# Pooled attention and a gated conv FFN: pooled keys and values in flat 128-row tiles, no conv on TensorE, some gates by sigmoid

## The chip, the cores and the metric

One core of a Trainium2 chip. The metric is the device time of one execution in microseconds; lower is better. The inputs are fp32 in HBM and the output is fp32; inside, the kernel works in bf16 with fp32 accumulation in PSUM.

## The reference

Eight batches, eight heads, 576 tokens, head size 64. Keys and values are averaged over groups of 8 tokens, so each head has 72 pooled keys. The attention output, with the heads side by side (512 wide), is the input of a gated feed-forward block.

```python
k_p = k.reshape(B, H, 72, 8, D).mean(axis=3)
v_p = v.reshape(B, H, 72, 8, D).mean(axis=3)
attn = softmax(q @ k_p.T / 8)                      # 576 x 72 per head
x = (attn @ v_p)                                   # heads side by side: B x 576 x 512
h = maximum(x @ w_in, 0)                           # 512 -> 1024
conv = cw[0]*h[s-1] + cw[1]*h[s] + cw[2]*h[s+1]    # along the tokens, per channel
out = (h * sigmoid(conv)) @ w_out                  # 1024 -> 512
```

## The kernel before

The kernel first makes a list of steps (`Planner.add`), each with an engine or a choice of engines, an estimated duration, a priority from `PARAMS`, what it reads and writes, and the PSUM slot that it takes. `Planner.order` then puts the steps in order, greedily, by those estimates, and the instructions are issued in just that order. Each engine works through its own queue in order. PSUM has three slots of two banks (tiles called psfA or psbA) and two slots of one bank (psfB, psbB). Gaps that the planner expects on TensorE in the first 60 us are filled with matmuls on zeros (`warm`, L266).

For each batch b the steps are these.

- **Loads.** `load_k`, `load_q` and `load_v` fetch with casting DMAs from GpSimd's queue (POOL). k_b holds the keys as 96 rows by 6, one row being the 8 tokens of a pooled key; v_b holds 72 rows by 8 heads. q_b holds the queries as flat tokens, 128 partitions of 36 tokens each. All three have two buffers, for even and odd batches. `weights_in` fetches w_in in four parts, `weights_out` w_out in two.
- **Pooling.** `attn_k` (L450 to L485) adds 512 elements to 256, 128 and 64 on DVE and transposes the sums into kT2; `attn_v` (L499 to L511) does the same additions for vaug, which has a 65th column of 8.0 that gives the row sums of the softmax.
- **Queries.** `attn_q` transposes q_b in 18 blocks (L523) and copies the result to qT (L529).
- **Scores.** `attn_s`: for each head two matmuls on 64 rows, of 72 by 288 each (L548), and one exp of 72 x 576 on ACT (L560); in batch 0 in three column parts, so 24 exps there and 56 in the other batches.
- **AV.** `attn_av`: for each of five token tiles eight matmuls of 65 columns (L580), the reciprocal of the row sums (L589), the normalisation xx on DVE (L593), four transposes (L607, with the permutation `perm` that undoes the token order) and a copy to xT (L613) by ACT or DVE.
- **mm1.** `mm1` (L652): eight matmuls of 288 columns for each of eight blocks f of 128 channels; relu on ACT (L658) into hT. Batch 0 is done in two column parts (L629, L636).
- **Conv and gate.** For two blocks at a time. A block in `PARAMS["off"]` goes through `conv_off`: the two outer taps are multiplied by DVE or ACT (L677, L675; the taps are divided by the middle one), two additions on DVE (L683, L689), a tanh on ACT (L694). The other ten blocks of the 64 go through `conv_pe`: six matmuls with diagonal matrices dw (L731) and a tanh from PSUM (L738). The gate is 0.5 (1 + tanh(z/2)): hT already holds half of h, DVE adds 1 (`tg1`, L711) and multiplies into gT (L717).
- **mm2.** Two batches share gT, 1152 tokens in nine tiles; `mm2` (L757) takes eight matmuls of 512 columns for each tile; ACT or DVE copies to osb (L784), and SyncE's queue (SP) stores (L789).

tanh, exp, relu and copy stand in one table of ACT, which is loaded once (L529 ACT_TABLE_LOAD). The batches overlap: loads run two batches ahead, attention one batch ahead of the feed-forward block.

Of the kernel before, what the change touches and what calls it, by code (L numbers as in the profile page):

```python
# [16 lines left out]
    "off": [(3, 5, 7), (0, 1, 2, 3, 6, 7), (0, 1, 2, 4, 5, 6, 7), (0, 1, 2, 3, 4, 5, 6, 7), (0, 1, 2, 3, 4, 5, 6, 7),  # L17
        (1, 2, 3, 4, 5, 6), (0, 1, 2, 3, 4, 5, 6, 7), (0, 1, 2, 3, 4, 5, 6, 7)],
    "acc": [0, 0, 0, 0, 0, 0, 0, 0],
    "bias": {"cp": 0.0323, "qT": -0.1231, "xt": 0.043, "kz": -0.1719, "oe": 0.0913},  # L20
    "ld0": [3.1628, -11.898, 6.0356, 17.1517],
    "ps0": [-11.2829, 7.5625, 41.439],
    "k": [-5.9822, -1.1583, -4.5734, -3.831, -6.5225, -2.7562, -4.2806, 15.1584],
    "q": [-0.1097, -9.2157, -9.8568, 3.1829, -4.6592, -3.0682, -1.5265, -8.4274],
    "v": [24.0425, -11.1807, 29.0547, 7.0183, 0.6186, 5.6688, -7.284, 39.6168],
    "s": [-6.9912, -16.7009, -0.9318, -0.6168, -3.6961, -1.0376, -0.9093, 1.2171],
    "ds": [3.8131, -0.3704, 0.0793, 0.7876, 1.3609, 0.4842, 0.2144, -4.845],
    "av": [-16.159, 1.1624, 8.4491, 2.1533, -4.2703, 4.1242, 4.9518, -37.1794],
    "conv": [4.8877, 4.2326, 2.864, 6.3276, 6.3981, 1.7124, -22.1068, 5.7406],
    "mm2": [25.5649, 32.1081, 13.6617, 18.3164, 23.0188, 19.8928, 18.2176, 20.5433, 24.0796, 28.9795, 21.0736,  # L30
        23.1375, 15.9486, 13.2485, 25.641, 4.8532, 20.6698, 5.4106, 10.0051, 16.9607],
# [3 lines left out]
ROW = 0.05  # L35
# [3 lines left out]
class Op:  # L39
    __slots__ = ("i", "name", "eng", "dur", "lat", "deps", "prio", "fn", "take", "give", "nbytes", "done", "users", "after")  # L40


class Planner:
# [4 lines left out]
    KINDS = {"qT": "BA", "kT": "BA", "xt": "BA", "cw": "BA", "o": "B", "sc": "A", "sc0": "A", "av": "A", "h": "A", "h0": "BA", "c": "A"}  # L48
    DMA_RATE = 330e3
# [3 lines left out]
    QUOTA = {"sc": 2, "o": 2}  # L53

# [6 lines left out]
    def add(self, name, eng, dur, fn, reads=(), writes=(), prio=0.0, lat=None, take=None, give=None, nbytes=0, after=None):  # L61
# [5 lines left out]
        o.fn, o.prio, o.take, o.give, o.nbytes = fn, prio, take, give, nbytes  # L67
# [8 lines left out]
        for k in writes:  # L76
            if k not in reads:
                self.writers[k] = [o.i]
                self.readers[k] = []
            else:  # L80
                self.writers[k] = [o.i]
                self.readers[k] = []
        deps.discard(o.i)
# [3 lines left out]
        o.done = None  # L87
        self.ops.append(o)
# [4 lines left out]
    def order(self):  # L93
# [14 lines left out]
        dma_free = 0.0  # L108
        busy = {}
        out = []  # L110
        while avail:
            best = None
            per = {}
            for i, t in avail.items():
# [9 lines left out]
                for e, d in o.eng.items():  # L124
                    s = max(st, free.get(e, 0.0))
                    f = s + d
                    if e == "ACT" and len(o.eng) > 1:
                        f += self.bias.get(o.name.split(".")[0][:2], 0.0)
                    if cand is None or f < cand[0]:
                        cand = (f, s, e)  # L130
# [10 lines left out]
            d = o.eng[e]  # L141
            del avail[i]
# [13 lines left out]
            if o.nbytes:  # L156
                dma_free = max(dma_free, s + d) + o.nbytes / self.DMA_RATE
                o.done = dma_free + (self.DMA_LAT if o.lat is None else o.lat)
            else:
                o.done = s + d + (self.LAT[e] if o.lat is None else o.lat) + self.SEM  # L160
# [12 lines left out]
        return out  # L173


@with_exitstack
def kernel(
# [19 lines left out]
    A = 16  # L197
    J = S // A
    KR = 96
    KT = H * Sp // KR  # L200

# [9 lines left out]
    perm = st("perm", [P, P], BF16)  # L211
    w_in = st("w_in", [P, n_dc, d_ff], BF16)
# [6 lines left out]
    dw = st("dw", [P, n_fb, 3, P], BF16)  # L219

    k_b = [st(f"k_b{i}", [KR, KT, 512], BF16) for i in range(2)]
    v_b = [st(f"v_b{i}", [Sp, H, 512], BF16) for i in range(2)]
    q_b = [st(f"q_b{i}", [P, J, D], BF16) for i in range(2)]
    kp1 = st("kp1", [KR, KT, 256], BF16)
    kp2 = st("kp2", [KR, KT, 128], BF16)
    ksum = st("ksum", [KR, KT, 2, D], BF16)
    vp1 = st("vp1", [Sp, H, 256], BF16)
    vp2 = st("vp2", [Sp, H, 128], BF16)
    vaug = [st(f"vaug{i}", [Sp, H, D + 1], BF16) for i in range(2)]
    kT2 = [st(f"kT2{i}", [P, H * Sp], BF16) for i in range(2)]  # L230
    qT = [st(f"qT{i}", [P, J // 2, P], BF16) for i in range(2)]
    attnT = [st(f"attnT{i}", [Sp, H, S], BF16) for i in range(2)]
# [3 lines left out]
    hT = [st(f"hT{i}", [P, n_fb, S + 4], BF16) for i in range(2)]  # L236
# [5 lines left out]
    OFF = PARAMS["off"]  # L242

# [13 lines left out]
    def warm(gap, x, prev):  # L257
        n = min(int((gap - 0.05) / 0.06), 100)
        if x is not None:
            t = pp.tile([P, 2 if x[0] == "A" else 1, 512], FP32, name=f"psw{x[0]}", tag=f"ps{x[0]}{x[1]}")[:, 0, 0:P]  # L260
        elif prev is not None and prev.take is not None and prev.take[0] == "sc0":
            t = slot(prev.take)[:, 0, 384:512]
        else:
            return
# [6 lines left out]
    def flat_tokens(src, b):  # L271
        return src[b].rearrange("h t d -> (h t d)").rearrange("(p e) -> p e", p=P)

    def rows_k(b):
        return k[b].rearrange("h (s p) d -> (h s) (p d)", p=8).rearrange("(t p) e -> p t e", p=KR)

    def rows_v(b):
        return v[b].rearrange("h (s p) d -> s h (p d)", p=8)
# [3 lines left out]
    def setup(b):  # L282
        pass

    QG = [(0, 4), (4, 12), (12, 18)]

    def load_q(b, parts, prio):
        m = b % 2
        for x, (c0, c1) in enumerate(QG if parts > 1 else [(0, J // 2)]):
            def fn(e, c0=c0, c1=c1):  # L290
                nc.gpsimd.dma_start(
                    out=q_b[m][:, 2 * c0:2 * c1, :],
                    in_=flat_tokens(q, b)[:, 2 * c0 * D:2 * c1 * D].rearrange("p (j d) -> p j d", d=D),
                )
            pl.add(f"ldq{b}.{x}", "POOL", 0.6, fn, writes=[("q", m, y) for y in ((x,) if parts > 1 else (0, 1, 2))],
                   prio=prio + (PARAMS["ld0"][x] if b == 0 else 0.0), nbytes=P * 2 * (c1 - c0) * D * 4)

    def load_k(b, prio):
        m = b % 2
        if b == 0:  # L300
            for i in range(2):
                def fn(e, i=i):
                    nc.gpsimd.dma_start(out=k_b[0][:, 3 * i:3 * i + 3, :], in_=rows_k(0)[:, 3 * i:3 * i + 3, :])
                pl.add(f"ldk0.{i}", "POOL", 0.75, fn, writes=[("kl", i)], prio=prio, nbytes=H * S * D * 2)
        elif PARAMS["acc"][b]:
            accumulate(b, "k", k_b, rows_k(b), prio)
        else:
            def fn(e):
                nc.gpsimd.dma_start(out=k_b[m], in_=rows_k(b))
            pl.add(f"ldk{b}", "POOL", 0.9, fn, writes=full_keys("k", m) + first(b, "k"), prio=prio, nbytes=H * S * D * 4)  # L310

    def half(b, full):
        x = 256 * ((b // 2 + 1) % 2)
        return full[b % 2][:, :, x:x + 256]

    def half_keys(b, name):
        return [(name, b % 2, (b // 2 + 1) % 2)]

    def full_keys(name, m):
        return [(name, m, 0), (name, m, 1)]  # L320

    def first(b, name):
        return [(name + "l", 0), (name + "l", 1)] if b in (2, 4) else []

    def accumulate(b, name, full, src, prio):
        n = 2 ** PARAMS["acc"][b]
        w = 512 // n
        keys = half_keys(b, name)
        for i in range(n):
            def fn(e, i=i):  # L330
                kw = {} if i == 0 else {"accum_op": OP.add}
                nc.gpsimd.dma_start(out=half(b, full)[:, :, 0:w], in_=src[:, :, i * w:(i + 1) * w], **kw)
            pl.add(f"ld{name}{b}.{i}", "POOL", 0.9, fn, reads=keys if i else [], writes=keys + (first(b, name) if i == 0 else []), prio=prio,
                   nbytes=int(H * S * D * 4 / n * 1.7), lat=5.0)

    def load_v(b, prio):
        m = b % 2
        if PARAMS["acc"][b]:
            return accumulate(b, "v", v_b, rows_v(b), prio)

        n = 2 if b == 0 else 1
        for i in range(n):
            def fn(e, i=i):
                c = slice(i * H // n, (i + 1) * H // n)
                nc.gpsimd.dma_start(out=v_b[m][:, c, :], in_=rows_v(b)[:, c, :])
# [493 lines left out]
    with tc.manual_schedule():  # L839
        prev = None  # L840
        for s, e, d, o in pl.order():
# [3 lines left out]
            if e == "PE":  # L845
                prev = o
# [31 lines left out]
```

## Time and profile before

| | |
|---|---|
| median of 3 runs | 210.06 us (209.61 to 210.35) |
| span of the profiled execution, first to last instruction | 208.8 us |
| time of the profiled execution itself | not listed apart from the three runs; the median is 1.26 us above the span |
| mean granted TensorE clock | 0.998 |
| busy PE, DVE, ACT, POOL | 200.5, 177.1, 169.9, 33.7 us |
| DMA packets, bytes | 20794, 26.02 MB |

The profile lists for every group of instructions its line in the kernel, what it writes and reads by the kernel's names, partitions by elements, the count, the busy time of the group and the mean duration of one in ns, then the idle time of the engine just before them and what ended it. PE is the matmul part of TensorE and PEld its weight loads. A digit in the slices is the busy share of an engine in a fortieth of the span, in tenths. The chain of waits goes back from the last instruction, at each step to what released it.

### The profile page before, as it was taken

Reading aid. Unit: us, or ns where it says so; the run is one execution under the profiler, and the core shown is the slowest. Engines: PE = TensorE matmul, PEld = TensorE weight load, DVE = VectorE, ACT = ScalarE, POOL = GpSimd, SP = SyncE. Lnnn points to the kernel's source line nnn. Section 1 sums busy time; section 2 is a strip of 40 time slices with the busy share of each in tenths; the row PEclk is TensorE's granted clock in tenths of the full one; section 3 lists DMA queues with packets and bytes.
Section 4 is the critical chain, followed back from the end, with each engine's and each line's share of the span. In section 5 each row is a group of like instructions: output and inputs, shape, how many; then the busy total and the mean of one; then the engine's idle time right before and its main releaser. Section 6 shows DMA issues by size and latency. Waiting matters only on the chain.

```text
span 208.8 us, 4761 instructions
## 1 busy us (share of the span) xinstructions
PE 200.5 (96%) x1917; PEld 135.2 (65%) x1917; DVE 177.1 (85%) x396; ACT 169.9 (81%) x305; POOL 33.7 (16%) x70
## 2 busy tenths in 40 slices
PE   8999899899999889999999999999999999999993
PEld 8987684687466666757565586547645767764432
DVE  1576589699999999999999999998997799999601
ACT  2056579969999997799999999999999878999431
POOL 7859951111303110010100100000000000000000
PEclk9999999999999999999999999999999999999999
DMA  5999999999999999309732280102202202102425
GB/s 76 160 198 206 204 206 210 201 198 195 155 142 224 170 249 186 77 5 144 166 119 102 33 179 6 53 0 100 96 9 100 104 0 104 50 0 102 154 100 201
DMA packets 20794, 26.02 MB, mean 125 GB/s; under 512 B 2444, under 2 KB 15268, under 8 KB 20772
## 3 DMA queue, kind: packets, MB, share of 16 engines
q0 software_dynamic: 15648, 16.26, 49.5%
q1 hardware_dynamic: 5124, 9.45, 12.0%
q8 instruction: 15, 0.25, 0.5%
q14 instruction: 7, 0.06, 0.1%
HBM read 32.52 MB, written 9.44 MB: 201 GB/s over the span
## 4 chain that ended last, share of the span: by engine, by line
PE 87%; ACT 8%; DVE 3%; issue 0%; ACTq 0%
PE psfB L757 30%; PE psfA L652 27%; PE psfA L548 5%; PE pswA L266 5%; ACT attnT L560 4%; PE psfA L580 4%; PE psfA L731 3%; PE psbB L607 3%; PE psfB L629 2%; PE psbB L523 2%; PE pswB L266 2%; DVE xx L593 1%; PE psbA L607 1%; PE psbB L480 1%; ACT osb L784 1%; ACT tg L738 1%
## 5 line engine op out<-in xcount | busy, mean ns | idle before, releaser
L757 PE MATMUL psfB<-w_out,gT 128*128 128x512 bf16 (+1 forms) x296 | 66.8, 373 | 0.5 <-ACT osb L784 0.5
L652 PE MATMUL psfA<-xT,w_in 128*128 128x288 bf16 x448 | 60.7, 286 | 0.3 <-ACT attnT L560 0.2
L652 PEld LDWEIGHTS <-w_in 128*128 128x128 bf16 x448 | 42.1, 98 | 12.7 <-issue 1.3
L757 PEld LDWEIGHTS <-gT 128*128 128x128 bf16 x296 | 27.7, 98 | 29.6 <-issue 1.3
L560 ACT ACTIVATE attnT<-psfA 72x576 bf16<-72x576 f32 (+3 forms) x80 | 39.8, 549 | 1.9 <-PE psfA L548 1.5
L658 ACT ACTIVATE hT<-psfA 128x576 bf16<-128x576 f32 x56 | 35.5, 652 | 6.3 <-PE psfA L652 5.9
L694 ACT ACTIVATE tg<-cv,cs 128x576 bf16<-128x576 bf16 x54 | 39.9, 777 | 0.8 <-DVE cv L689 0.8
L677 DVE TENSOR_SCALAR cv<-hT,cr 128x576 bf16<-128x576 bf16 x78 | 26.0, 361 | 3.3 <-ACT hT L658 3.1
L593 DVE TENSOR_TENSOR xx<-psfA,rr 128x512 bf16<-128x512 f32 x40 | 26.8, 681 | 0.1
L784 ACT COPY osb<-psfB 128x512 f32<-128x512 f32 x31 | 17.9, 584 | 9.0 <-PE psfB L757 8.7
L717 DVE TENSOR_TENSOR gT<-tg,hT 128x1152 bf16<-128x1152 bf16 x32 | 23.9, 747 | 0.1
L675 ACT ACTIVATE cv<-hT,cr 128x576 bf16<-128x576 bf16 x30 | 22.7, 781 | 0.2
L689 DVE TENSOR_TENSOR cv<-cv 128x1152 bf16<-128x1152 bf16 (+1 forms) x30 | 20.5, 684 | 0.0
L683 DVE TENSOR_TENSOR cv<-cv,hT 128x1152 bf16<-128x1152 bf16 (+1 forms) x30 | 20.4, 681 | 0.0
L548 PE MATMUL psfA<-qT,kT 64*72 64x288 bf16 (+3 forms) x160 | 19.0, 277 | 1.4 <-ACT attnT L560 0.8
L266 PEld LDWEIGHTS <-zero 128*128 128x128 bf16 x216 | 15.2, 110 | 2.6 <-DVE zero L365 1.0
L548 PEld LDWEIGHTS <-kT 64*72 64x72 bf16 x160 | 7.8, 107 | 13.4 <-issue 10.2
L711 DVE TENSOR_SCALAR tg<-tg 128x1152 bf16<-128x1152 bf16 x32 | 14.3, 448 | 1.7 <-ACT tg L694 1.2
L580 PE MATMUL psfA<-vaug,attnT 72*128 72x65 bf16 x320 | 15.5, 194 | 0.3 <-ACT attnT L560 0.3
L529 ACT COPY qT<-psbB 128x512 bf16<-128x512 bf16 (+2 forms) x10 | 7.1, 744 | 9.6 <-PE psbB L523 9.6
L580 PEld LDWEIGHTS <-attnT 72*128 72x128 bf16 x320 | 13.5, 98 | 1.5 <-issue 0.5
L607 PEld LDWEIGHTS <-xx 128*128 128x128 bf16 x160 | 10.7, 97 | 4.8 <-DVE xx L593 1.1
(67 smaller groups left out, 218.4 us busy)
## 6 DMA issues: line engine op xcount, KB each, us to landing
out_dram<-osb SPq DMA_DIRECT2D x15, 512.0 KB, 3.3
k_b<-in_k_dram POOLq DMA_DIRECT2D x7, 576.0 KB, 12.1
q_b<-in_q_dram POOLq DMA_DIRECT2D x7, 576.0 KB, 10.6
v_b<-in_v_dram POOLq DMA_DIRECT2D x7, 576.0 KB, 9.8
out_dram<-osb SPq DMA_DIRECT2D x5, 256.0 KB, 2.0
w_in<-in_moe_w_in_dram POOLq DMA_DIRECT2D x4, 256.0 KB, 10.2
w_out<-in_moe_w_out_dram POOLq DMA_DIRECT2D x2, 512.0 KB, 18.1
k_b<-in_k_dram POOLq DMA_DIRECT2D x2, 288.0 KB, 6.2
```

The lines of the kernel that those rows point to most:

```text
L266: nc.tensor.matmul(out=t, lhsT=zero[:, 0:P], rhs=zero[:, 0:P], start=True, stop=True)
L548: nc.tensor.matmul(out=t[:, par, :], lhsT=kT2[m][64 * par:64 * par + 64, h * Sp:(h + 1) * Sp], rhs=qT[m][64 * par:64 * par + 64, 2 * c0:2 ...
L560: nc.scalar.activation(out=attnT[m][:, h, :].rearrange("p (c i x) -> p i c x", i=2, x=32)[:, :, c0:c1, :], in_=view().rearrange("p i (c x) ...
L580: nc.tensor.matmul(out=a[:, h // 4, c:c + D + 1], lhsT=attnT[m][:, h, u0:u0 + 128], rhs=vaug[m][:, h, :], start=True, stop=True)
L593: nc.vector.tensor_tensor(out=xx[i3].rearrange("p (g h e) -> p g h e", g=2, h=4), in0=av_view()[:, :, :, 0:D], in1=rr[i3].rearrange("p (g ...
L652: nc.tensor.matmul(out=t[:, i, 0:HC], lhsT=w_in[:, c, f * P:(f + 1) * P], rhs=xT[m][:, c, i * HC:(i + 1) * HC], start=(c == 0), stop=(c == ...
L658: nc.scalar.activation(out=hT[m][:, f, 2:S + 2].rearrange("p (i x) -> p i x", i=2), in_=slot(key)[:, :, 0:HC], func=ACT.Relu, scale=0.5)
L675: nc.scalar.activation(out=cv[y][:, kk // 2, z, :], in_=src, func=ACT.Copy, scale=s)
L677: nc.vector.tensor_scalar(out=cv[y][:, kk // 2, z, :], in0=src, scalar1=s, scalar2=None, op0=OP.mult)
L694: nc.scalar.activation(out=tg[i3][:, f % 2, :], in_=cv[y][:, 0, z, :], func=ACT.Tanh, scale=cs[:, f:f + 1])
L717: nc.vector.tensor_tensor(out=gT[(b // 2) % 2][:, fs[0]:fs[0] + 2, o:o + S], in0=tg[i3], in1=hT[m][:, fs[0]:fs[0] + 2, 2:S + 2], op=OP.mult)
L757: nc.tensor.matmul(out=a[:, 0, 0:cols.stop - cols.start], lhsT=g[:, c, t * P:(t + 1) * P], rhs=w_out[:, c, cols], start=(c == 0), stop=(c ...
```

## The change

- Keys and values are pooled as flat rows (head, token): 576 rows in five tiles of 128, the last half empty. The loads of k and v are split in four full tiles and a tail of 64 rows (batch 0 in three transfers).
- Queries are loaded as 72 partitions by 8 heads by 8 tokens into a single q_b, and then regrouped to q2, token before head: by two copies on DVE (or ACT) for batches 0 to 3 and 7, by eight SyncE DMAs of 128-byte pieces for batches 4 to 6 (`PARAMS["rg"]`). Transposes take two heads of 72 tokens, 32 for a batch.
- kz is a block layout of kT for pairs of heads with zeros between. A score tile holds 128 flat keys; one or two pairs of heads are accumulated into it, each by matmuls of 512 and 64 columns with 128 rows. There are five exps of 128 x 576 for a batch, batch 0 included.
- In AV a flat tile of keys can hold rows of up to three heads: vblk holds the pooled values three times, each times a mask (made on POOL) that is one for the rows of that head. Six matmuls of 65, 130 or 195 columns replace eight of 65.
- Every conv block goes off TensorE. The conv matrices dw are no longer made.
- The order of tokens in xT is the natural one, so the copies read and write runs of 128.
- ACT's gate is a sigmoid where the planner has the sigmoid table in place, else 0.5 (1 + tanh): `PARAMS["sw"]` and `Planner.SWITCH` decide. In the built order 42 of the 64 gates are sigmoids, and ten table loads stand on ACT, nine of them inside the stream. `tg1` (now 0.5 x + 0.5) is left out where all the gates of a pair are sigmoids; relu is no longer halved.
- w_in is fetched in two parts. The planner has another model of the DMA queues and an order of loads written out (`PARAMS["seq"]`), and all priorities are new.

The core of the diff:

```diff
+    q_b = st("q_b", [PR, H, TP, D], BF16)
+    q2 = st("q2", [PR, TP, H, D], BF16)
...
+    def regroup(b, pr):
+        n = 2 if b == 0 else 1
+        if PARAMS["rg"][b] == "D":
+            for h in range(0, H, 4):
+                def fn(e, h=h):
+                    copy_on(e)(out=q2[:, :, h:h + 4, :], in_=q_b[:, h:h + 4].rearrange("p h i d -> p i h d"))
+                pl.add(f"qg.{b}.{h}", {"DVE": 0.6, "ACT": 1.8}, 0, fn, reads=[("ql", h // 4)], writes=[("q", 0, h + z) for z in range(4)],
+                       prio=pr + 0.01 * h)
+            return
+        for h in range(H):
+            def fn(e, h=h):
+                nc.sync.dma_start(out=q2[:, :, h, :], in_=q_b[:, h])
...
+        mk = mask.rearrange("p t x d -> p (t x d)")
+
+        def fn(e):
+            nc.gpsimd.memset(mk, 1.0)
+        pl.add("mask0", "POOL", 0.5, fn, writes=["mask"], prio=-50)
+        for x, (base, sg) in enumerate(((Sp, 1), (-1, -1))):
+            def fn(e, base=base, sg=sg):
+                nc.gpsimd.affine_select(out=mk, in_=mk, compare_op=OP.is_ge, fill=0.0, base=base,
+                                        pattern=[[-16 * sg, NT], [-Sp * sg, 3], [0, D + 1]], channel_multiplier=sg)
...
+        def fn(e):
+            nc.vector.tensor_tensor(out=vs, in0=vp2[:, :, 0:D], in1=vp2[:, :, D:2 * D], op=OP.add)
...
+            nc.vector.tensor_tensor(out=vblk[m][:, :, :, 0:D], in0=vs.unsqueeze(2).to_broadcast([P, NT, 3, D]),
+                                    in1=mask[:, :, :, 0:D], op=OP.mult)
...
+    PAIRS = [(0,), (0, 1), (1, 2), (2, 3), (3,)]
...
+            for y, (n0, n1) in enumerate(((0, 512), (512, S))):
+                for c in PAIRS[t]:
+                    w = kz[m][:, 256 * c + (P if t > c else 0):256 * c + (P if t > c else 0) + P]
+                    r = qT[m][:, c]
...
+                    nc.tensor.matmul(out=a[:, y, 0:n1 - n0], lhsT=w, rhs=r, start=c == PAIRS[t][0], stop=c == PAIRS[t][-1])
...
-            for h in range(H):
-                c = (h % 4) * (D + 1)
-                nc.tensor.matmul(out=a[:, h // 4, c:c + D + 1], lhsT=attnT[m][:, h, u0:u0 + 128],
-                                 rhs=vaug[m][:, h, :], start=True, stop=True)
...
+            for s, x0, x1, g, c in ((0, 1, 3, 0, 0), (1, 0, 3, 0, 1), (2, 0, 1, 0, 3), (2, 1, 3, 1, 0), (3, 0, 3, 1, 1), (4, 0, 1, 1, 3)):
+                nc.tensor.matmul(out=a[:, g, c * w:(c + x1 - x0) * w], lhsT=attnT[m][:, s, u0:u0 + 128],
+                                 rhs=vblk[m][:, s, x0:x1, :].rearrange("p x d -> p (x d)"),
...
-                out=xT[m].rearrange("p c (a j) -> p c a j", j=J)[:, :, :, 8 * t:8 * t + w],
-                in_=slot(key2)[:, 0, 0:512].rearrange("p (c a j) -> p c a j", c=4, a=A)[:, :, :, 8 - w:8],
...
+            copy_on(e)(out=xT[m][:, :, 128 * t:128 * t + w],
+                       in_=slot(key2)[:, 0, 0:512].rearrange("p (c a) -> p c a", c=4)[:, :, 0:w])
...
+                half = not pl.ops[gi[z0]].mode
+                nc.scalar.activation(out=tg[i3][:, zs[z0]:zs[z0] + z1 - z0, :], in_=cv[y][:, 0, z0:z1, :],
+                                     func=ACT.Tanh if half else ACT.Sigmoid, scale=cs[:, g:g + 1] if half else cn[:, 1, g:g + 1])
...
+                nc.vector.tensor_scalar(out=t, in0=t, scalar1=1.0, scalar2=0.5, op0=OP.add, op1=OP.mult)
```

And in the parameters:

```diff
-    "off": [(3, 5, 7), (0, 1, 2, 3, 6, 7), (0, 1, 2, 4, 5, 6, 7), (0, 1, 2, 3, 4, 5, 6, 7), (0, 1, 2, 3, 4, 5, 6, 7),
-        (1, 2, 3, 4, 5, 6), (0, 1, 2, 3, 4, 5, 6, 7), (0, 1, 2, 3, 4, 5, 6, 7)],
...
+    "sw": [0, 1, 1, 1, 0, 1, 0, 1],
...
+    "rg": "DDDDSSSD",
```

## The prediction

> **What bounds the kernel now.** I read the page first: busy shares, then the slices.
>
> ```profile
> span 208.8 us, 4761 instructions
> PE 200.5 (96%) x1917; PEld 135.2 (65%) x1917; DVE 177.1 (85%) x396; ACT 169.9 (81%) x305; POOL 33.7 (16%) x70
> DVE  1576589699999999999999999998997799999601
> ACT  2056579969999997799999999999999878999431
> PE 87%; ACT 8%; DVE 3%; issue 0%; ACTq 0%
> ```
>
> One digit is 5.2 us. DVE is nearly full from the ninth digit (42 us) to 195 us, ACT not far behind. PE's busy time counts matmul latency and warm-up matmuls on zeros, so I price PE by starts. The chain in order of time does that:
>
> ```profile
> 22.46 0.55 PE psfA L266 x7
> 23.02 0.65 PE psfB L629 x4
> ...
> 33.81 4.35 ACT attnT L560 x8
> ...
> 48.93 1.96 PE psfA L652 x16
> ...
> 78.02 1.73 PE psfB L757 x8
> ...
> 185.71 13.39 PE psfB L757 x62
> 199.17 0.59 ACT osb L784
> ```
>
> So 128x512 costs 0.2165 us (1.73/8), 128x288 0.1225 (1.96/16), 0.42 ns a column. The first real layer-1 matmul (mm1) starts at 22.85 by the timeline, its last layer-1 matmul ends at 185.71; then only mm2 is left. The groups by form give ACT and DVE:
>
> ```profile
> L694 ACT ACTIVATE tg<-cv,cs 128x576 bf16<-128x576 bf16 x54 | 39.9, 777 | 0.8 <-DVE cv L689 0.8
> L560 ACT ACTIVATE attnT<-psfA 72x576 bf16<-72x576 f32 x56 | 33.3, 646 | 0.2 <-PE psfA L548 0.2
> L677 DVE TENSOR_SCALAR cv<-hT,cr 128x576 bf16<-128x576 bf16 x78 | 26.0, 361 | 3.3 <-ACT hT L658 3.1
> L711 DVE TENSOR_SCALAR tg<-tg 128x1152 bf16<-128x1152 bf16 x32 | 14.3, 448 | 1.7 <-ACT tg L694 1.2
> L499 DVE TENSOR_TENSOR vp<-v_b 72x2048 bf16<-72x2048 bf16 x7 | 8.5, 1215 | 0.0
> L529 ACT ACT_TABLE_LOAD x1 | 1.3, 1283 | 0.7 <-PEq L862 0.7
> ```
>
> Neighbours overlap: eight exps take 4.46 us, the last one whole, so 0.535 each against 0.646; a tanh pair 1.44, so 0.665. I take 0.115 off each ACT mean and 0.075 off each DVE mean (0.448 starts the next after 0.37). Counts by order times these prices give the work before: PE 174.2 (mm1 62.7, mm2 62.3, transposes 19.6, scores 12.3, AV 10.0, conv 7.4), DVE 174.3, ACT 161.1 us. PE holds 150.5 of it between 22.85 and 185.71, 162.9 us long: 12.4 us of gaps, about 4 of them before 44.6 us.
>
> **The change, engine by engine.** Counts come from the built order.
>
> PE. Sixty conv matmuls go: -7.4. Scores become 64 pairs of 512 and 64 columns, 64 x 0.247 = 15.8, against 112 x 0.0925 + 1.9 = 12.3: +3.5. AV becomes 40 tiles of 130, 195 and 65 columns twice, 0.35 each by column, 14.0 against 320 x 0.031 = 10.0: +4.0. The 256 transposes of q at 72 columns (0.034) cost 8.7 against 144 x 0.057 = 8.3; those of k +0.2. PE: 175.0, +0.8. So taking the conv off PE only pays for the flat tiles.
>
> ACT. Exps 80 to 40: 21.3 against 34.8, -13.5. Nine table loads inside the stream at 1.28: +11.5; of the 64 gates 42 use sigmoid, priced like tanh from SBUF (+1.3 in all). Copies of xT 14 to 33: +8.3. Copies of kz +2.4, of osb -1.8, the rest -0.2. Sum +8.0: 169.1.
>
> DVE. Outer-tap multiplies 78 to 99: +6.0; their adds, all 1152 wide now: +6.3. The gate's add 32 to 11: -7.8. Copies of xT 26 to 7: -5.9; of osb +2.4; of k -0.5. Pooling on 128 rows, 1280, 640 and 320 elements where 2048 and 1536 were: -7.2 by the slope (1.215-0.422)/1536 us. New is the masked copy vblk, 960 elements, eight times. No row has its two strides at once; by the same slope 0.65, by twice the element time 1.15. The old vaug write, also 65 apart, cost 0.422 like a plain 512, so I take 0.65: +4.6. New too are ten regrouping copies of q, 2048 elements: 0.70 by the slope from the multiply of 576 to the add of 1152, 1.2 by the tensor_tensor row of 2048. It reads one tensor out of SBUF, as the multiply and the add do: 0.70, +6.2. Small things +0.5. DVE: 178.9, +4.6. Its set-up memsets and the first batch's two regroupings, about 3.5 us, fall before 20 us, where DVE idles; so the load afterwards hardly grows.
>
> Queues. On POOL k0 and v0 come in three transfers and q0 in two, then two mask passes (0.29 for 128 columns, so 1 to 2 us each for 975), and w_in stands behind them, issued near 12 us instead of 6.6. It is not needed before 21 us, and the 1.77 MB ahead of it keep the DMA busy to about 13; without that cover mm1 waits for it, some 2 us. q_b is one buffer now, so the load of the next q, and v's behind it on POOL, wait for the regrouping of this one; POOL already waits 24.5 us for kp to free k_b by the waits, and nothing on the chain is released by it: 0, as long as loads run a batch ahead. On SP 24 regrouping transfers serve batches 4 to 6, each batch's eight behind an output store (issue 0.4 us by its row), and later stores behind them. No row shows 128-byte pieces in bulk. Hidden while q comes a batch early: 0; a late one costs the stores and psfB's copies up to 3 us. I take 0 and keep 3.
>
> **Start: -1.5.** Before, the last q piece is transposed at 12.35 and AV waits for V and exps until 18.02. After, q and k are the same bytes: 12.4, regrouping 0.65, sixteen transposes and their copy 1.1, scores of the third tile 0.6, three exps 1.7 (3 x 0.535 + 0.115): 16.5. V lands near 15.2 as before, pooling and masking 1.6: 16.8. From AV to mm1 there were 4.8 us, with 0.7 behind exps of the old column split, which are gone. Mm1 starts at 21.0 to 21.5, 1.5 earlier. **PE work to the last mm1: -2.2**: 148.3 by the order. **Gaps: -1.6**: the next batch's exp run (33.81) holds PE up and is three exps shorter. Bounds: half of all gaps gone (-5.4), or ACT cannot keep up (+9, below). **Tail: +1.7**: after the last mm1 stand 96 full-width equivalents, 20.8 us, for 88, 19.05.
>
> Sum -3.6: span 205.2. The median of the runs (210.06; 209.61 to 210.35) stands 1.26 above this profile's span, which has no time of its own on the page. Forecast **206.5 us**, 1.7% faster.
>
> **Rivals.**
> *ACT becomes the bound (slower).* Between first and last relu ACT did 144.3 us of work in 163.8, 88.1%. After it has 149.1, and my forecast leaves 160.0: 93.2%. For: xT's copies sit on ACT, and a table load holds up the relu that frees psfA, so mm1 behind it. Against: the windows between 90 and 150 us show ACT 94 to 100% busy. The time is 22.2 (first relu) plus the stretch, less 1.8 from the last mm1 to the end of its relu, plus 24.8 to the end (208.8 - 185.7 + 1.7), plus the 1.26. At 88.1% the stretch takes 169.2 and the time is 215.7, at 90% 212.2; at 91% it is 210.3, no change: there it decides.
> *A switch costs twice its load (slower).* If ACT has to run empty around each, nine more loads' time, 11.5, make ACT's work 160.6; at 93.2% that is 172.3 us and 218.8. The only row is at the start, with nothing ahead of it, so it cannot show this. The Trainium skill (ScalarE: Activation LUTs, What ACT_TABLE_LOAD costs) says exactly that: about 1283 ns to load, where the trace agrees, and some 1380 ns of drain. By its figures, as an estimate, the nine drains would add 12.4 us to ACT and bring the time to about 220.
> *The unseen DVE copies run at their slow ends (slower).* Seven vblk and eight regroupings after the start, 0.5 more each: +7.5 on a full engine, 214.0.
> *The flow gets smoother (faster).* Fewer, larger exps and no conv in psfA's slots halve the gaps after 44.6 us too, 8.3: -4.2, 202.3.
> *It comes out even*: gaps grow by about 3.5. The change does do what it says, but 22 of the 64 gates stay tanh.
>
> **Numbers.** Forecast case 0.42 (its own range 204 to 209); smoother 0.15; even 0.08; ACT bound 0.20; slow copies 0.09; double switches 0.06. Measurement can tell some 0.3% (0.63 us) from no change. Faster 0.57, same 0.08, slower 0.35. The range reaches from the smoother case to the slow copies: 201.5 to 214.0; beyond lie the double switches and half of the ACT case, with a little below.
>
> **What would show it.** Right: AV before 17.5 us, the last mm1 ending near 180, about 25 us to the end; ten table loads of 1.28; ACT over 92% busy from 25 to 180; regrouping near 0.7, vblk near 0.65. Wrong: last mm1 after 184; PE waits on psfA released by ACT at table loads; gaps after each load; DVE rows of 1.2 for the new copies; stores queued behind regrouping.

## The result: 5% slower, and the profile after

The changed kernel takes 221.05 us (median of 4 runs, 219.93 to 223.84), the kernel before 209.84 beside it: a ratio of 1.0515, 95% interval 1.0463 to 1.0566. The forecast was 206.5. Some executions fall in a slower state at a lower granted clock (here the one of 223.84, and the profiled one of `e1_two_q` below); the medians hold them, the ratios do not. The profiled execution of the changed kernel took 220.29 us, 1.7 more than its span.

The head of the page, two rows of slices, and the first line of its chain:

```profile
span 218.6 us, 4711 instructions
PE 198.0 (91%) x1837; PEld 137.7 (63%) x1851; DVE 183.7 (84%) x413; ACT 176.4 (81%) x298; POOL 39.0 (18%) x60
...
DVE  4798498998999999976789959999999978999500
ACT  2045899999999999994879965997899888999631
...
PE 42%; DMA 22%; ACT 14%; POOL 7%; DVE 7%; issue 4%; SPq 0%; POOLq 0%; DVEq 0%; ACTq 0%
```

The span grew by 9.8 us, and PE, DVE and ACT fill no larger share of it than they filled of the old one. DMA, which does not appear in the chain before, holds 22% of this one: 6% is the load of k for batch 1, from 13.5 to 26.2 us, the rest lies between 78 and 130 us. The slices agree: digits 18 to 25 (93 to 137 us) have dips on DVE and ACT that the kernel before did not have. The waits of POOL and DVE, then of SyncE (total, times, longest), and the chain in order of time (start, duration) show what happens there:

```profile
POOL q_b L347 <- DMA q<-q_b: 50.2, 3, 17.2
POOL q_b L347 <- DVE q L356: 18.7, 2, 13.4
...
DVE kp L506 <- DMA k_b<-in_k_dram: 4.5, 4, 1.4
```

```profile
SPq L362 <- DMA q_b<-in_q_dram: 27.3, 3, 9.8
```

```profile
77.83 0.65 SPq L362
...
78.53 2.47 DMA q<-q_b
...
81.77 1.07 POOL q_b L347
82.84 0.88 POOL v_b L374
...
84.26 0.75 POOL k_b L374
85.01 10.73 DMA k_b<-in_k_dram
...
95.83 0.83 DVE kp L506
...
98.17 2.48 DMA q<-q_b
...
101.51 0.85 POOL q_b L347
102.36 0.76 POOL v_b L374
103.12 9.96 DMA v_b<-in_v_dram
...
118.57 2.71 DMA q<-q_b
```

This is a loop that nothing in the kernel before had. The last piece of a regrouping lands, q_b is free, and POOL issues the next load of q (81.77). SyncE waits for that load: it lands 8 us after its issue, and the next regrouping starts at 89.78. Its eight pieces take 9 us to issue, the last lands 2.5 us after its issue began (98.17), and the load after it goes out at 101.51. One turn takes 20 us (78.5, 98.2, 118.6); there are three regroupings of this kind, for batches 4 to 6. The loads of v and k stand behind q in POOL's queue, so they wait with it. The chain runs through them: they land 10 to 11 us after their issue, and the pooling on DVE waits for k. The load of q for the last batch goes out at 122.1 us; in the kernel before it went out at 100.3. SyncE's own timeline has the issue of the eight pieces:

```profile
69.79 9.53 SPq L362 DMA_DIRECT2D q<-q_b  x8
...
89.78 9.19 SPq L362 DMA_DIRECT2D q<-q_b  x8
...
110.66 8.97 SPq L362 DMA_DIRECT2D q<-q_b  x8
```

That is 1.15 us a piece on the mean (0.80 at the median, 2.63 at most), where an output store takes 0.37 at the median. The windows put most of the loss in the same place (length; busy time of each engine with its instructions; clock, DMA share, GB/s). Before and then after:

```profile
90.00:135.00 45.00, 44.82 (x420) 28.65 (x419) 44.22 (x97) 43.90 (x76) 2.19 (x3) 1.00 0.42 94
```

```profile
90.00:135.00 45.00, 40.08 (x390) 28.48 (x392) 37.30 (x81) 36.52 (x63) 5.61 (x8) 0.96 0.87 154
```

DVE, which had worked for 44.2 of these 45 us, works for 37.3, and PE works 4.7 us less. A smaller loss lies ahead of the loop: from 21 to 45 us PE works for 19.4 of 24 us, before for 22.2, while ACT works for 22.5, before for 19.4.

### The profile page after: what moved, and what is told of

It reads as the page before. It is cut to its first block, busy times and chain, and to the rows that moved or that the text cites. A ratio compares the mean times of both kernels' runs of the same rounds, so it can differ in the third digit from the quotient of the medians.

```text
span 218.6 us, 4711 instructions
## 1 busy us (share of the span) xinstructions
PE 198.0 (91%) x1837; PEld 137.7 (63%) x1851; DVE 183.7 (84%) x413; ACT 176.4 (81%) x298; POOL 39.0 (18%) x60
## 4 chain that ended last, share of the span: by engine, by line
PE 42%; DMA 22%; ACT 14%; POOL 7%; DVE 7%; issue 4%; SPq 0%; POOLq 0%; DVEq 0%; ACTq 0%
PE psfB L829 19%; PE psfA L689 16%; DMA k_b<-in_k_dram 11%; DMA v_b<-in_v_dram 5%; DMA q_b<-in_q_dram 4%; DMA q<-q_b 4%; ACT attnT L603 3%; ACT tg L751 3%; PE psfA L598 2%; ACT osb L858 2%; PE psfA L618 2%; ACT xT L652 2%; POOL v_b L374 1%; POOL q_b L347 1%; POOL k_b L374 1%
## 5 line engine op out<-in xcount | busy, mean ns | idle before, releaser
L751 ACT ACTIVATE tg<-cv,cn 128x576 bf16<-128x576 bf16 x42 | 31.2, 773 | 4.4 <-DVE cv L743 4.2
L603 ACT ACTIVATE attnT<-psfA 128x576 bf16<-128x576 f32 x40 | 24.4, 662 | 2.5 <-PE psfA L598 2.5
L738 DVE TENSOR_TENSOR cv<-cv,hT 128x1152 bf16<-128x1152 bf16 x32 | 24.0, 749 | 0.2
L743 DVE TENSOR_TENSOR cv<-cv 128x1152 bf16<-128x1152 bf16 x32 | 23.9, 749 | 0.0
L598 PE MATMUL psfA<-qT,kz 128*128 128x64 bf16 (+1 forms) x128 | 21.0, 297 | 0.6 <-DVE qT L577 0.6
L618 PE MATMUL psfA<-vblk,attnT 128*128 128x130 bf16 (+2 forms) x240 | 19.1, 222 | 2.7 <-ACT hT L695 1.2
L618 PEld LDWEIGHTS <-attnT 128*128 128x128 bf16 x240 | 15.7, 98 | 4.8 <-issue 3.3
L598 PEld LDWEIGHTS <-kz 128*128 128x128 bf16 x128 | 10.9, 102 | 10.2 <-issue 2.2
L751 ACT ACTIVATE tg<-cv,cs 128x576 bf16<-128x576 bf16 x22 | 17.0, 807 | 0.3 <-DVE cv L743 0.3
L652 ACT COPY xT<-psbB 128x512 bf16<-128x512 bf16 (+1 forms) x25 | 13.7, 558 | 4.4 <-PE psbB L646 4.2
```

Of the source, the lines that this page charges most:

```text
L598: nc.tensor.matmul(out=a[:, y, 0:n1 - n0], lhsT=w, rhs=r, start=c == PAIRS[t][0], stop=c == PAIRS[t][-1])
L603: nc.scalar.activation(out=attnT[m][:, t, :], in_=slot(key).rearrange("p i x -> p (i x)")[:, 0:S], func=ACT.Exp, scale=1.0 / 64.0)
L618: nc.tensor.matmul(out=a[:, g, c * w:(c + x1 - x0) * w], lhsT=attnT[m][:, s, u0:u0 + 128], rhs=vblk[m][:, s, x0:x1, :].rearrange("p x d -> ...
L738: nc.vector.tensor_tensor(out=cv[y][:, 0, 0:n, :], in0=cv[y][:, 0, 0:n, :], in1=h_at(2), op=OP.add)
L743: nc.vector.tensor_tensor(out=cv[y][:, 0, 0:n, :], in0=cv[y][:, 0, 0:n, :], in1=cv[y][:, 1, 0:n, :], op=OP.add)
L751: nc.scalar.activation(out=tg[i3][:, zs[z0]:zs[z0] + z1 - z0, :], in_=cv[y][:, 0, z0:z1, :], func=ACT.Tanh if half else ACT.Sigmoid, scale ...
```

## The experiments

Each kernel was timed beside the kernel before, and what two kernels differ by is worked out from their ratios to it, times 209.8 us. Unless it is said otherwise the order of instructions is that of the kernel edited.

### One q buffer, the transfers, or the copies

A second q_b needs room, so the pooling is written in place; `e1_inplace` does only that.

```diff
-    q_b = st("q_b", [PR, H, TP, D], BF16)
+    q_b = [st(f"q_b{i}", [PR, H, TP, D], BF16) for i in range(2)]
-    kp1 = st("kp1", [P, NT, 256], BF16)      # kp2 and vp1 too
+    # sums written over k_b and v_b            (this alone: e1_inplace)
```

> Control for the next run. The pooled sums kp1, kp2 and vp1 are written over the loaded rows in k_b and v_b, which frees 6.3 KB of a partition; the order of all instructions stays that of the changed kernel. The buffers of k and v come free one or two DVE steps later. Late-loads theory and table-switch theory alike: no change, 221 us, at most 1 us more.

> As the control, and q_b gets a second buffer; order unchanged. Late loads (q_b has one buffer and stands between v and k in POOL's queue, so each of the loads of batches 5, 6 and 7 waits for the SyncE regrouping of the batch before: POOL waits 50.2 us for it): POOL's waits for DMA q<-q_b go, k of batches 5 to 7 lands 15 us or more earlier, the idle time of DVE and PE between 90 and 135 us goes: 213 us (210 to 216). Table switches bound the kernel: no change, 221 us.

Measured: in place alone 222.08 us (ratio 1.049, 1.0427 to 1.0554), as the changed kernel; with two buffers 217.43 (1.0348, 1.031 to 1.0386), 3.0 us less, where the theory had 8. SyncE now starts its pieces 7 to 9 us earlier, and they hold its queue for longer:

```profile
62.31 14.52 SPq L359 DMA_DIRECT2D q<-q_b  x8
...
80.44 20.03 SPq L359 DMA_DIRECT2D q<-q_b  x8
...
102.56 15.63 SPq L359 DMA_DIRECT2D q<-q_b  x8
```

These are 1.8 to 2.5 us a piece on the mean against 1.15 (at the median 1.55 against 0.80, the longest 7.69). Loads of the next batch are under way then; that these are what slows the pieces was not tested. So the second buffer opens the loop, and the longer issues may well be what takes part of it back. The next kernel takes the pieces away and leaves one buffer, and one later does both.

```diff
-                nc.sync.dma_start(out=q2[:, :, h, :], in_=q_b[:, h])
+                if h % 4 == 0:
+                    nc.vector.tensor_copy(out=q2[:, :, h:h + 4, :], in_=q_b[:, h:h + 4].rearrange("p h i d -> p i h d"))
```

> The 24 SyncE transfers that regroup q of batches 4 to 6 become two DVE copies of 2048 elements a batch, at the same place in the order; q_b still has one buffer. DVE gets 6 x 0.6 = 3.7 us more. Late loads: the loop of load, regrouping and next load loses some 9 of its 20 us (eight issues of 1.15 us and a landing of 2.5 us become 1.3 us), three times; 215 us (211 to 218). Table switches bound: 221 to 224 us.

> Pooling written in place to make room, two q_b buffers, and the regrouping of batches 4 to 6 on DVE instead of SyncE, so that neither the single buffer nor the small transfers are left; only the sixteen DVE copies are. Theory (with the transfers gone the copies' own time on a DVE that was busy 44.6 of 45 us between 90 and 135 us is what remains): the second buffer is worth under 1 us more, 214.8 to 216.5 us. Rival (the late loads of q, k and v still cost, by the 37.0 us that POOL waited for the DVE regrouping): 212 to 214 us, near the 212.3 us of the kernel without regrouping.

Measured: DVE copies with one buffer 215.79 us (1.0285, 1.0246 to 1.0323), with two 214.85 (1.0248, 1.0211 to 1.0286). The loop and its transfers are worth 5.6 us together, give or take 1.3. The second buffer alone brought 3.0 and the copies alone 4.8, which is 7.8 and not 5.6, so in part they cured one thing. With one buffer and DVE copies the window is full again on DVE, and PE still has not its old 44.82:

```profile
90.00:135.00 45.00, 42.38 (x424) 30.13 (x426) 44.60 (x98) 40.65 (x72) 5.71 (x8) 1.00 0.62 119
```

Next the regrouping is left out for batches 1 to 7, or put on GpSimd, or done by the load:

```diff
-                    copy_on(e)(out=q2[:, :, h:h + 4, :], ...)      # and the SyncE pieces
+                    if b == 0: copy_on(e)(...)                     # e5_no_regroup
+                    (copy_on(e) if b == 0 else nc.gpsimd.tensor_copy)(...)   # e6_pool_regroup
+                for hh in range(H):                                # e9_direct_q, b > 0, two q2
+                    nc.gpsimd.dma_start(out=q2[m][:, :, hh, :], in_=rows_q(b)[:, hh, :].rearrange("p (i d) -> p i d", i=TP))
```

> Left out: the regrouping of q for batches 1 to 7, by SyncE and by DVE alike; the transposes read what batch 0 left in q2, so q's values are wrong from batch 1 on. Order unchanged, q is still loaded. The theory now: the changed kernel loses first to the load loop (5 us, as the runs with a second q_b and with DVE copies showed), and what is left is DVE's own work. Then this kernel has neither, its DVE work is 178.9 - 4.9 = 174 us, that of the kernel before, and it comes out level: 210 us (207 to 213). If something else slows it (table switches, the tail), it stays above 214.

> The regrouping of batches 1 to 7 moves to two copies of 2048 elements a batch on GpSimd, which is busy 18% of the span; at 1.2 ns an element (its mask pass of 975 took 1.18 us) 2.5 us each. One q_b, order otherwise unchanged; in POOL's queue the next loads stand behind the copies. Load loop and DVE work theory: nearly the kernel without regrouping, 211 us (208 to 215). If the copies are much slower than that, or hold DVE up, 216 us or more. Table-switch theory: 221 us.

> Batches 1 to 7 have no regrouping at all: eight GpSimd loads a batch put q from DRAM straight into the grouped layout, 72x8x64 each, into two buffers (pooling in place makes room); batch 0 stays. Theory (regrouping, wherever it is done, is the cost, and the small pieces hurt only because they come after the load): about the time without regrouping, 212 to 214 us. Rival (pieces of 128 bytes are slow on the queue as such, 9 to 20 us a batch as on SyncE, and k and v stand behind them): 216 us and more, with DVE waiting for k_b.

Without regrouping, where the scores of batches 1 to 7 are made from batch 0's queries: 212.32 us (1.013, 1.0077 to 1.0183). That is 2.5 us below DVE copies with two buffers, for 14 copies fewer, and 8.1 below the changed kernel; it is still slower than the kernel before. On GpSimd: 228.4 (1.0871, 1.0806 to 1.0936), the slowest regrouping, and not only because a copy there is long. Groups of that kernel:

```profile
L732 DVE TENSOR_SCALAR cv<-hT,cr 128x576 bf16<-128x576 bf16 x99 | 40.6, 442 | 4.0 <-ACT hT L674 2.6 <-ACT tg L752 0.7 <-ACT hT L696 0.6
...
L356 POOL COPY q<-q_b 72x2048 bf16<-72x2048 bf16 x8 | 16.6, 2104 | 32.5 <-PE psbA L572 15.2 <-DMA q_b<-in_q_dram 10.3 <-PE psbB L572 7.0
```

GpSimd needs 2104 ns where DVE took 683, and DVE's own multiply rises from 368 to 442 ns on the mean. The mean hides two kinds: the median is 364 ns, but the five of the 99 that overlap a copy on GpSimd in time take 1393 to 1998. All of DVE is busy for 196.6 us against 183.7, with eight copies fewer to do. By the load: 219.24 (1.0443, 1.0371 to 1.0515), on the rival's side. The small pieces now stand in POOL's own queue in front of v and k, as the chain in order of time shows:

```profile
69.75 0.96 POOL q L348 x2
...
72.66 0.76 POOL k_b L376
73.42 10.33 DMA k_b<-in_k_dram
83.83 0.82 DVE k_b L508
```

Between 75 and 90 us PE is busy for 9.63 of 15, in the changed kernel for 14.80.

### The table switches

```diff
-    func=ACT.Tanh if half else ACT.Sigmoid, scale=cs[:, g:g + 1] if half else cn[:, 1, g:g + 1])
+    func=ACT.Tanh, scale=cs[:, g:g + 1] if half else cn[:, 1, g:g + 1])
```

> All gates call tanh, so the nine table loads inside ACT's stream go and nothing else changes; where the changed kernel had sigmoid, the gate is left at tanh of the full argument without the 0.5 x + 0.5. Table switches bound: 11.5 us or more less, 209 us. Late loads: ACT is full only up to 90 us, and the load loop sets the pace after it; 2 us less (0 to 4), 219 us.

> Left out: regrouping as in the kernel without it, and the nine table loads in ACT's stream (all gates call tanh, without 0.5 x + 0.5 where sigmoid stood). With the load loop gone the switches can show themselves. If they matter once loads are early: 6 to 10 us less than the kernel without regrouping. If DVE is what bounds: within 2 us of it.

Measured: 219.94 us (1.0503, 1.0465 to 1.054) in the changed kernel, which its own interval cannot tell from 1.0515; 210.87 (1.0047, 1.0025 to 1.007) where the regrouping is out as well, 1.7 us below the same kernel with its loads. Nine loads hold 11.5 us of ACT and cost 0.2 and 1.7 us of the time, each give or take 1.3. On ACT itself they can be seen to take no more than their own time. Groups of the changed kernel, then ACT's chain around one load:

```profile
L751 ACT ACT_TABLE_LOAD x5 | 6.4, 1283 | 0.1
...
L603 ACT ACT_TABLE_LOAD x4 | 5.1, 1283 | 0.1
```

```profile
65.33 1.28 ACT L751
66.63 2.77 ACT tg L751 x4
69.41 0.95 ACT osb L858 x2
70.37 1.28 ACT L603
71.67 1.75 ACT attnT L603 x3
```

ACT's next instruction starts 0.01 to 0.02 us after the load's end, and the last copy before the second load ends at 70.36; it is so at all nine. What is lost beside the 1283 ns is the usual overlap of neighbours. The drain of some 1380 ns that the Trainium skill (ScalarE: Activation LUTs, What ACT_TABLE_LOAD costs) adds to each switch is not in these rows.

### What the sigmoid brings

```diff
         plan = pl.order()
+        for o in pl.ops:
+            if o.kind == "gate":
+                o.mode = False          # all tanh; tg1 for every pair again
```

> The changed kernel with two q_b buffers and DVE regrouping (214.85 us), order kept, with the sigmoid part undone: all gates tanh, no table loads in the stream, and the gate's add back in 21 more pairs, 7.8 us of DVE. Theory (DVE's price of 0.83 on 7.8 us, less some 1.4 for the loads): 219 to 221 us, so that the sigmoid part of the change had gained 5 us. Rival (the adds fit into DVE's gaps, the loads are what shows): 213 to 215 us.

Measured: 220.37 us (1.0481, 1.0442 to 1.052) against 214.85: 4.9 us more, as the theory said. So the sigmoid, with its table loads, is a part of the change that pays. Put into the kernel before, for 8 and for 11 of its 32 pairs, it did not:

```diff
-    func=ACT.Tanh, scale=cs[:, f:f + 1])
+    func=ACT.Sigmoid if (b, f // 2) in SIG else ACT.Tanh, scale=cs[:, f:f + 1])   # relu unhalved, tg1 left out for SIG
```

> The kernel before, order kept, with sigmoid in place of tanh for the eight pairs of blocks of batches 6 and 7, all of whose gates follow the last exp: one table load of 1.28 us on ACT, and eight of the 32 DVE adds of 0.37 gone (3.0 us). Theory (DVE sets the pace, 0.83 us of time for a us of DVE, and the load costs 0.1 to 0.2 us as the nine others did): 1.5 to 2.5 us less, 207.5 to 208.5. Rival (after 145 us, with no exps left, PE is full: 40.00 of 40 us between 150 and 190, and DVE's relief there is worth nothing): 209.5 to 210.2 us.

> As the kernel beside it, with three more pairs (4.3, 5.0 and 5.1) between two exps on sigmoid: two more table loads, 2.6 us of ACT, and three more adds gone, 1.1 us of DVE. Theory (the DVE price and cheap loads): 0.5 to 0.9 us below the kernel beside it. Rival (ACT, 14.79 of 15 us busy between 135 and 150, pays for its loads): 0.5 to 2 us above it.

Measured: 211.37 us (1.0078, 1.006 to 1.0096), slower than both the theory and its rival had it, and 212.94 (1.0157, 1.0142 to 1.0173), 1.6 above the first, as its rival said. Here one load costs at least its 1.28 us. The chain of the first of the two:

```profile
165.75 0.40 ACT hT L658
166.31 1.28 ACT L694
167.60 1.44 ACT tg L694 x2
169.04 0.48 ACT osb L786
169.56 1.89 PE psfB L759 x8
```

The load stands ahead of two gates and a copy of osb, and mm2 waits for the slot that this copy frees. By ACT's timelines the relu in front of the load starts at 165.66, in the kernel before at 166.77; the gates behind it start at 167.60, before at 167.30. So 1.4 us are lost there. PE is busy for 13.89 us of the 15 from 165 to 180, for 15.00 in the kernel before. As far as these runs go, a load's price is that of its place: next to nothing where the plan left a place for it, all of it where PSUM is waited for. The eight adds that were left out after the last exp, 3 us of DVE, bought nothing that can be seen; that PE is full there is the reason offered, and it was not tested.

### Taking the conv off TensorE

```diff
-    "off": [(3, 5, 7), (0, 1, 2, 3, 6, 7), ...
+    "off": [(0, 1, 2, 3, 4, 5, 6, 7)] * 8,          # e8: the kernel before
```

> The kernel before, with one part of the change alone: all conv blocks off TensorE, so the planner orders anew. By the counts of its order PE's work falls by 7.4 us to 166.8, DVE's grows by 10.6 to 184.9 and ACT's by 4.4 to 165.5. DVE bounds: slower by about 8, 218 us (213 to 221). PE bounds, as the chain of the kernel before suggests with 87%: faster by 3 to 6, 205 us.

> The kernel with DVE regrouping, with the conv blocks that the kernel before had on TensorE put back there (the same list of blocks; 20 blocks, 60 conv matmul pairs); pooling in place for room; the order of work is planned anew by the kernel's planner, with priorities set for the other list. Theory (DVE is the full engine, PE has gaps of some 19 us): 12 us of DVE's multiplies and adds leave for 7.4 us of PE work, and the time falls below the 215.8 us of DVE regrouping alone, to 210 to 214 us. Rival (PE's starts are what counts, or psfA's slots): 7.4 us more PE work shows, 217 to 223 us.

Measured: 227.18 us (1.0725, 1.0686 to 1.0763) for the kernel before with all conv off TensorE; 236.96 (1.13, 1.1246 to 1.1354) for the changed kernel with it put back and DVE regrouping. The list has ten blocks and sixty matmuls. Both times lie beyond what either theory gave. Both kernels were planned anew with priorities that were set for the other list, so neither tells the price of the work from that of a bad order: in the second, 4% of the chain is GpSimd making dw, and another 4% is the load of w_in. They settle nothing about the conv.

Three kernels that keep the order can at least price PE and DVE in the kernel before:

```diff
-            for kk in range(3):                      # conv_pe, 60 matmuls
+            for kk in (1,):                          # e11: 20
...
+            for _ in range(2):                       # e12: tg1 twice; e13: both edits
                 nc.vector.tensor_scalar(out=tg[i3], in0=tg[i3], scalar1=1.0, scalar2=None, op0=OP.add)
```

> The kernel before, order kept, with the two outer taps of the conv on TensorE left out (40 of 60 conv matmuls of 288 columns, 4.9 us of PE starts); their part of the result is left out. Theory A (my prediction's: PE, at 87% of the chain, sets the end): 205 to 206 us. Theory B (DVE sets the pace and PE waits for it): 208.5 to 210 us.

> The kernel before, order kept, with the gate's add of 1152 elements done twice in each of 32 blocks: 32 x 0.37 = 11.8 us more DVE work, about what the outer taps moved to DVE cost; the gate's value is changed by it. Theory A (PE sets the end, DVE has room beside it): 210 to 214 us. Theory B (DVE is full between 42 and 195 us): 218 to 222 us.

> Both edits of the two kernels beside it, so that PE has 4.9 us less and DVE 11.8 us more, order kept. Theory A (PE): 206 to 211 us. Theory B (DVE): as with the DVE load alone, 217 to 222 us, within 1 us of it.

Measured: 4.9 us less of PE, 208.62 us (0.9921, 0.9897 to 0.9944), 1.7 us less. 11.8 us more of DVE, 220.03 (1.0458, 1.041 to 1.0505), 9.6 more: 0.8 us for a us. Both, 219.92 (1.0447, 1.0402 to 1.0492): with DVE loaded, the relief of PE can no longer be seen (0.2 us, give or take 1.4). One window of 140 us, of the kernel before and of the one with the load on DVE:

```profile
45.00:185.00 140.00, 138.29 (x1282) 91.28 (x1281) 135.11 (x299) 130.10 (x221) 8.60 (x12) 1.00 0.50 106
```

```profile
45.00:185.00 140.00, 132.91 (x1213) 85.67 (x1225) 137.28 (x307) 124.30 (x209) 8.99 (x12) 1.00 0.49 104
```

DVE had 4.9 us to spare in 140, and with the load PE and ACT idle instead. PE's 138.29 looks fuller than DVE's 135.11, but PE's busy time counts each matmul to its modelled end: mm2's have a mean of 373 ns and start 217 ns apart. The count of PE's starts had found 12.4 us of gaps.

## Why the prediction was wrong, point by point

**The account.** Of the 10.8 us (1.0515): the loop of one q_b with SyncE's pieces 5.6 (to the kernel with two buffers and DVE copies), DVE's 14 regrouping copies 2.5, the nine table loads 1.7, and 1.0 for all the rest together. The first three differences carry 1.2 to 1.4 us of uncertainty each, the last 0.5. That 1.0 is a balance and not a small effect. With the sigmoid part as one term, the 4.9 us that it gains, the conv off TensorE, the flat tiles, the xT copies on ACT and the new order together cost 10.8 - 5.6 - 2.5 + 4.9 = 7.6 us, by this reckoning: more than the loop, and no run here takes it apart. The prediction's own DVE terms, without the gate's adds and the regrouping, come to 4.6 + 7.8 - 6.2 = 6.2 us. At the 0.8 measured in the kernel before, up to 5.0 of the 7.6 would be DVE's, an estimate; the sum had given DVE's work no price in time.

**"0, as long as loads run a batch ahead"** is the step that failed, and with it "I take 0 and keep 3" for SyncE. The prediction named the condition and did not test it: 5.6 us stand where it had 0. The load of q and its regrouping take turns in the one q_b, and neither can start before the other has ended. A load of 8 to 9 us, 9.2 us of issues and a landing of 2.5 make a turn of 20 us of what had been prefetch, and v and k stand behind q in POOL's queue. That POOL waits long is no sign of it: after 20 us it idles 82.0 us ahead of loads, and 79.1 in the kernel before. What changed is that the last loads of k and q go out 11 and 22 us later, and that DVE waits 4.5 us for k, PE 1.9 us for the regrouped q. The eight pieces had no price in the sum; the only row was the 0.4 us of a store, and they took 1.15 each. The copies on DVE were priced near what they took, but their 6.2 us were taken to cost no time; the 14 of the kernel without SyncE's pieces cost 2.5.

**PE as the bound** failed too. The sum was made of PE's starts and gaps because the chain read "PE 87%". The chain names what came last, and where three engines are within a few per cent of full that is no bound: with 4.9 us of PE taken away the time fell by 1.7, with 11.8 us put on DVE it rose by 9.6. "DVE is nearly full from the ninth digit" was the right line, and the sum did not use it. That DVE's load "afterwards hardly grows" is borne out: of its 183.7 us 14.4 lie before 20 us, of the 177.1 before the change 9.6, so 169.3 stand behind against 167.5. At 0.8 those 1.8 us would have cost 1.4, an estimate, in a kernel that was forecast 3.6 faster.

**Terms.** The two prices bounded for want of a row came out: the changed kernel's groups have both.

```profile
L356 DVE COPY q<-q_b 72x2048 bf16<-72x2048 bf16 x10 | 6.6, 683 | 2.3 <-DMA q_b<-in_q_dram 2.3
L557 DVE TENSOR_TENSOR vblk<-vs,mask 128x960 bf16<-128x960 bf16 x8 | 5.2, 650 | 0.1
```

0.683 for 0.70, 0.650 for 0.65; the rival of slow copies falls. The 0.70 was luck in part. It comes out only if the multiply goes in at 0.286, its overlap taken off, and the add at its full 0.448; by both means, 0.361 and 0.448, the slope gives 0.58. Tail: 25.5 us from the end of the last mm1 to the end of the span, where about 25 was forecast. Start: mm1 at 21.98 for 21.0 to 21.5, AV at 17.93 for 16.8; 0.5 to 1.1 us late. Gaps: the last mm1 ends like this

```profile
192.14 0.98 PE psfA L689 x8
193.12 5.61 PE psfB L829 x26
```

so the stretch from the first mm1 is 171.1 us, and with the 148.3 of work counted from the order 22.8 are gaps: 10.4 more than before, where -1.6 was forecast and +9 was the upper bound. With the start at -0.9 (21.98 after 22.85) for -1.5 and the tail at +2.4 (25.5 after 23.1) for +1.7, the gaps are the term of the sum that holds the miss. Without regrouping and without table loads the stretch goes from 22.53 to 184.37, 161.8 us, and the gaps are 13.5 if the count of PE's work holds; the hoped-for 1.6 us of smoother flow did not come.

**The rivals.** ACT as the bound of the whole: no, ACT works for 36.52 of the 45 us from 90 to 135, fewer than before, and 11.5 us of loads taken off it bring 0.2 and 1.7. From 21 to 45 us it may be: there ACT works for 22.5 of 24 us and PE for 19.4, and without regrouping and loads PE still works for 19.8; this was not tested. A switch that costs twice its load had given 218.8 to 220, close to what came out; without the table loads the kernel is hardly faster, so the number was right for a reason that is not there.

**Open.** The 7.6 us of the conv, the flat tiles and the order above. The price of a us of DVE is not one number: 0.8 for the gate's adds, 2.5 us for 14 copies of 0.61 (0.3), which fall partly where DVE waits anyway. What the conv alone did in the changed kernel was not taken apart in that kernel's order.

## What to carry to other kernels

Where several engines are near full, the chain's top engine need not be the bound: take a little work from one and put a little on another, in the kept order, and read the price of a us of each before pricing a trade between them. When a double buffer becomes single, write down the turn (how long the load takes, who empties the buffer and how fast, what is queued behind the reload) and compare its length with the time of a batch. A number that fits a rival does not confirm it until its cause is taken away.

## What the runs showed of the hardware

- A DMA of 72 x 8 pieces of 128 bytes from SBUF to SBUF holds SyncE's queue for 0.80 us at the median of 24 and 1.15 on the mean, in the kernel with two q buffers for 1.55 and 2.1; the longest took 2.63 and 7.69, and what held them is open. The last of eight lands 2.5 us after its issue began. The Trainium skill (DMA: Bandwidth & Descriptors, Why small descriptors are slow) says that SBUF-to-SBUF transfers do not pay the penalty of small pieces, and gives 78% of the link's best for a remote transfer of 1 MB in 128-byte packets. Here eight transfers of 72 KB in 9.2 us are 64 GB/s, and SyncE was issuing for all of that time, which that figure does not speak of.
- A GpSimd copy of 72x2048 takes 2104 ns on the mean of eight and 2053 of six. Beside these 14 DVE's one-input multiply rises from 368 to 442 ns on the mean, vblk's from 650 to 858, the second add into cv from 749 to 828 and the first not at all (749 and 748). The medians stay (364, 654, 749 and 749); the longest are 1998, 2350, 2435 and 759. So a few instructions wait, for up to about the length of a copy. The Trainium skill (GPSIMD Engine Reference, 1. Specifications) has the two engines share SBUF interfaces, with contention where DVE runs in a two-port mode or has two SBUF inputs. The rows of vblk and of the second add, with two inputs, agree; the first add has two inputs and keeps its time, but met a copy only once; in which mode the multiply runs, no row says.
- A table load in the stream takes 1283 ns on the mean of each group, and at none of the nine does ACT idle for more than 0.02 us before or after it.
- In the two 15 us windows where PE idles most its granted clock is lower: 0.89 from 30 to 45 us (PE busy for 11.05 of 15) and 0.90 from 90 to 105 (12.17), where the kernel before had 1.00 in both (13.80 and 15.00).
